# Three chained layers on one core: the last block product of each Strassen run moved into the next run, raw weights in a ring

## Chip, cores and metric

One core of one Trainium2 chip. The metric is the device time in microseconds (us) of one execution, median of the runs; shorter is better.

## What is computed

Sigmoid attention over 24 heads, then a gated MLP with an RMS norm in front, then a second MLP. All inputs and the output are float32 (the weights reach the chip as 8-byte words, two 32-bit halves each):

```
scores = q @ k.T / 8 - log(448);  a = 1 / (1 + exp(-scores));  o = a @ v      # 2 x 12 heads, 448 x 64
x  = o as (896, 768)
xn = x / rms(x) * rms_g
y  = (silu(xn @ w_gate) * (xn @ w_val)) @ w_out        # 768 -> 1536 -> 768
out = (silu(y @ w2_in)) @ w2_out                       # 768 -> 2048 -> 768
```

## The kernel before

Attention runs first (to about 71 us); its matmuls are issued by `scores` (L382) and `attend` (L409). Then come the products, each float32 product made of three fp32r matmuls of 128x128 by 128x448 (high by high, low by high, high by low, `PASSES`). Most products go through Strassen's algorithm in Winograd's form on 2x2 blocks, with seven block products instead of eight. A call of `strassen` (its matmuls are issued by `group`, L798) is one **run**: seven groups of nine matmuls in the order `A11, S1, S2, A12, S3, S4, A22` (names of the weight side). They go to three PSUM banks: `x` takes A11, S2, S3 and A22, `y` takes S1 and S4, `z` takes A12. In between, the partial sums in a bank have to be read before the next group adds to it: ScalarE saves the bank after A11 (`save`, L830, tile `s0`) and S2 waits for that; it saves it after S2 (`s2`) and S3 waits for that; VectorE's add (L836) reads it after S3 and A22 waits for that. Runs: `g1` to `g5` and `v1` to `v5` (gate and value of the first MLP), `i1` to `i7` (second MLP in). At the end of a run without gating, ScalarE applies silu (L865): to block 11, to blocks 00 and 01 together, and to block 10 out of PSUM.

The products with w_out are `o0`, `o1`, `o2` (`mixed`): a plain part (`product`, L747, two double banks `a` and `b`) and a Strassen part on the same banks. `i0` is `mixed` too, `e0` to `e1b` are the second MLP out.

**Weights.** A slab of weights (`raw`, 128x768 words, 768 KB, or 512 KB for a short one) is loaded by SP's queue (L239) into one of two buffers (pool `wraw`). ScalarE rebuilds the exponent into a tile `f` (`exponent`, L257, one of three buffers), ScalarE or VectorE shifts the tail in place (`tail_act`, L265), VectorE merges both (`merge`, L269), and the buffer is free again. Then the Strassen sums are formed (L687 to L709), and each block is split into a high part on ScalarE (L245) and a low part on VectorE (L248), both in a ring of nine tiles `w`. `mac_steps` gives this in seven steps, A22 last.

**What sets the order.** From the norm on, the program is a list of jobs in a `Plan`; when the kernel is built, `Plan.run` plays it with costs per job, takes for each engine the job that is due first among those whose inputs are ready, and writes the instructions in that order. Each engine then executes its list in order. A load counts there as landed `LAG["S"]` = 4.4 us after it is issued, whatever its size; the job behind it is not put on an engine earlier.

```
            e = scalar(1.08 * n, lambda: exponent(s, spare if alt else None), [r], take="alt" if alt else "f")
            end = now + j.cost + LAG[e]
```

Of the kernel before, what the change touches and what calls it, by code (L numbers as in the profile page):

```python
# [39 lines left out]
LAG = {"A": 0.0481, "D": 0.081, "P": 0.165, "S": 4.4, "G": 5.0}  # L40
HOP = {"A": 0.516, "D": 0.3833, "S": 0.4, "G": 0.5}
# [18 lines left out]
class Job:  # L60


    def __init__(self, eng, cost, fn, deps, take, need):
# [3 lines left out]
        self.due, self.ready, self.left = 1e9, 0.0, 0  # L67
        for d in self.deps:
            d.users.append(self)
# [6 lines left out]
class Plan:  # L76
# [37 lines left out]
    def run(self, busy):  # L114
# [8 lines left out]
        for j in reversed(self.jobs):  # L123
            if j.eng != "P":
                j.due = min([u.due for u in j.users + j.users_of_gift], default=1e9) - WAIT[j.eng] * j.cost - LAG[j.eng] - HOP[j.eng]
# [30 lines left out]
        while left:  # L156
# [6 lines left out]
            while again:  # L163
                again = False
                for e in ("P", "D", "A", "S", "G"):
# [17 lines left out]
                    end = now + j.cost + LAG[e]  # L183
# [14 lines left out]
def tile_attention_two_mlps(  # L198
# [12 lines left out]
    wraw = ctx.enter_context(tc.tile_pool(name="wraw", bufs=2))  # L211
# [23 lines left out]

    def load(s):
        raws[s] = wraw.tile([P, 2 * SLAB], U32, tag="raw", name=f"raw{s}")
        n = 2 * wide(s)
        nc.sync.dma_start(raws[s][:, :n], wd[s].bitcast(U32)[:, :n])  # L239

    def load_next():
        load(order.pop(0))
# [7 lines left out]
    def words(s):  # L250
        return raws[s][:, : 2 * wide(s)].rearrange("p (n two) -> p n two", two=2)
# [329 lines left out]
    plan = Plan({"raw": 0, "f": 1, "ring": RING - 8, "alt": 1, "sum": 1, "ps": 0, "one": 0})  # L581
# [57 lines left out]
    wjob = {}  # L639

    def weight_front(s, act_z, tiles, alt=False):
# [3 lines left out]
        r = None if s in LOADED else plan.add("S", 0.4, lambda: load(s), take="raw")  # L645
# [3 lines left out]
        return plan.frees("raw", dve(n, lambda: merge(s), [e, z]))  # L649
# [11 lines left out]
    def weight_mac(macs, act_z, alt=True, early=False):  # L661

        todo = [mac_steps(s, n, act_z, alt, early) for s, n in macs]
        for _ in range(8):
            for t in todo:
                next(t)

    def mac_steps(s, n, act_z, alt, early):
# [24 lines left out]

        s1 = dve(hw, first, m, take=None if inside else "sum")
# [24 lines left out]
        if one:  # L719
            plan.frees("alt" if alt else "f", l1, l2, l4, l5, l6)  # L720
        else:
            if not inside:
                plan.frees("sum", l1, s2)
            plan.frees("f", *[l2, l5] + ([l1] if inside else []))
            plan.frees("alt" if inside else "f", l4, l6)
# [95 lines left out]
    def strassen(name, s, book, fdep, dst, own=None, gate=None):  # L821
# [26 lines left out]
        v1 = save(1, by, g2_)  # L848
        g3 = g(bx, "S2", deps=[v0])
# [4 lines left out]
        g5 = g(bx, "S3", deps=[v2])  # L854
        a11, o11 = output(1, 1, bx, 1, [g5, v1] + ([a00] if dst.fresh else []))
        g6 = g(by, "S4", stop=True, deps=[v1])
        a01, o01 = output(0, 1, by, 2, [g6, v2] + ([a00] if dst.fresh else []))
        by.read_by(v1, a01)
        g7 = g(bx, "A22", stop=True, deps=[a11])
        sdone[:3] = o00, o11, o01  # L860
        if gate:
            e = dve(S, lambda: tt(dst()[:, 1, 0], bx(), dst()[:, 1, 0], ALU.mult), [g7] + gate)
            bx.read_by(e)
            return [o00, o11, o01, e]
        silu = lambda out_, in_: nc.scalar.activation(out_, in_, AF.Silu)  # L865
        d11 = scalar(S, lambda: silu(dst()[:, 1, 1], dst()[:, 1, 1]), [o11])
        d0 = scalar(NT, lambda: silu(dst()[:, 0], dst()[:, 0]), [o00, o01])
        d10 = scalar(S, lambda: silu(dst()[:, 1, 0], bx()), [g7, a00], psum=True)
        bx.read_by(d10)
        return [d11, d0, d10]  # L870

    def mixed(
# [48 lines left out]
        if ahead:  # L921
            a00 = add(0, bz, [g4, v0], 0, 0)
# [655 lines left out]
```

## Time and profile before

| | |
|---|---|
| median of 3 runs | 523.17 us (521.27 to 523.77) |
| the profiled execution | 522.38 us |
| its span, first to last instruction | 520.4 us |
| PE (matmul) busy | 515.3 us, 99%, 2654 matmul records |
| PEld (weight load) busy | 442.7 us, 85% |
| VectorE (DVE) busy | 471.3 us, 91% |
| ScalarE (ACT) busy | 380.5 us, 73% |
| granted TensorE clock | 1.00 |

PE is busy all the time by this page, so a share of busy time tells nothing of a change in the order. What does is the time of one group of nine matmuls in the chain of waits, and whether the weight loader (PEld) had to wait for another engine ahead of a group. The engines' own lists in order of time then tell what that engine did instead.

### The profile page before, as it was taken

The page shows a single profiled execution, that of the slowest core. Times are in us where ns is not written, and L with a number is a line of the kernel's source. Part 1 is how long each engine was busy: PE and PEld are TensorE (multiplying, and loading weights), DVE is VectorE, ACT ScalarE, POOL GpSimd, SP SyncE. Part 2 cuts the span into 40 slices and gives each one's busy share as a digit, 9 for nine tenths or more (in the row PEclk, how much of TensorE's full clock was granted, in tenths as well). Part 3 has the DMA queues.
Part 4 walks back from the last instruction along what each step waited for, and adds up shares of the span by engine and source line. Part 5 has one row for each costly group of instructions (what it writes and reads, how often), then busy time and mean ns, then how long its engine had stood idle before and what let it go on. Part 6 is the DMA issues. An engine that isn't in the chain of part 4 may idle for free.

```text
span 520.4 us, 7479 instructions
## 1 busy us (share of the span) xinstructions
PE 515.3 (99%) x2654; PEld 442.7 (85%) x2654; DVE 471.3 (91%) x883; ACT 380.5 (73%) x677; POOL 13.5 (3%) x28
## 2 busy tenths in 40 slices
PE   9999999999999999999999999999999999999996
PEld 4444469999999999999999999999998999999996
DVE  6799999999999888799989989999988899999992
ACT  6876754787888676876777868998888887778730
POOL 0000000000000000000000000000010101111000
PEclk9999999999999999999999999999999999999999
DMA  8774111033332353411442362333355242555531
GB/s 319 276 248 162 62 62 60 1 122 122 121 123 88 103 209 108 162 42 40 163 161 82 125 217 84 122 121 123 135 186 195 97 134 95 169 199 200 187 123 71
DMA packets 18116, 70.51 MB, mean 136 GB/s; under 512 B 2464, under 2 KB 5024, under 8 KB 18080
## 3 DMA queue, kind: packets, MB, share of 16 engines
q1 hardware_dynamic: 16400, 64.32, 35.8%
q0 software_dynamic: 1536, 5.51, 3.1%
q8 instruction: 20, 0.33, 0.3%
q10 hardware_dynamic: 144, 0.23, 0.1%
q14 instruction: 16, 0.13, 0.1%
HBM read 64.54 MB, written 5.51 MB: 135 GB/s over the span
## 4 chain that ended last, share of the span: by engine, by line
PE 99%; DVE 0%; issue 0%
PE av L409 7%; PE sc L382 6%; PE g L747 3%; PE e2S L798 3%; PE v L747 3%; PE e1x L798 2%; PE o2x L798 2%; PE o1x L798 2%; PE e0bx L798 2%; PE o0x L798 2%; PE e2a L798 2%; PE i6x L798 1%; PE g2x L798 1%; PE i7x L798 1%; PE e0x L798 1%; PE e1bx L798 1%
## 5 line engine op out<-in xcount | busy, mean ns | idle before, releaser
L265 ACT ACTIVATE raw<-raw 128x768 int32<-128x768 uint32 (+1 forms) x70 | 57.4, 825 | 12.9 <-DMA raw<-in_w 9.4
L269 DVE SCALAR_TENSOR_TENSOR f<-f,raw 128x768 uint32<-128x768 uint32 (+1 forms) x65 | 58.4, 900 | 7.5 <-ACT f L257 5.9
L245 ACT ACTIVATE w_S<-f 128x384 fp32r<-128x384 f32 (+1 forms) x90 | 44.7, 497 | 23.0 <-DVE f L698 7.7
L257 ACT ACTIVATE f<-raw 128x768 f32<-128x768 f32 (+1 forms) x65 | 55.7, 859 | 4.4 <-DVE w_S L248 2.6
L248 DVE TENSOR_TENSOR w_S<-f,w_S 128x384 fp32r<-128x384 f32 (+1 forms) x90 | 47.3, 526 | 4.7 <-ACT w_S L245 4.3
L391 ACT ACTIVATE a<-sc,logs 128x896 f32<-128x896 f32 x42 | 39.1, 1008 | 15.3 <-PE sc L382 15.3
L245 ACT ACTIVATE w_A<-f 128x384 fp32r<-128x384 f32 (+1 forms) x84 | 41.2, 500 | 7.2 <-PE o2y L747 1.8
L248 DVE TENSOR_TENSOR w_A<-f,w_A 128x384 fp32r<-128x384 f32 (+1 forms) x84 | 43.8, 533 | 1.8 <-ACT w_A L245 1.8
L409 PE MATMUL av<-a,vr 128*64 128x448 f32 (+1 forms) x192 | 35.4, 552 | 0.0
L409 PEld LDWEIGHTS av<-a,vr 128*64 128x64 f32 (+1 forms) x192 | 10.4, 135 | 21.3 <-issue 20.3
L382 PEld LDWEIGHTS sc<-ks 64*128 64x128 f32 x204 | 18.3, 186 | 10.5 <-issue 5.5
L382 PE MATMUL sc<-ks 64*128 64x448 f32 x204 | 24.7, 380 | 0.0
L1131 DVE TENSOR_TENSOR g<-g 128x448 f32<-128x448 f32 x32 | 19.4, 620 | 0.1
L245 ACT ACTIVATE w_S<-s 128x384 fp32r<-128x384 f32 x24 | 12.5, 520 | 6.0 <-PE g L747 3.1
L709 DVE TENSOR_TENSOR f<-f 128x384 f32<-128x384 f32 (+1 forms) x30 | 15.8, 525 | 0.2
L245 ACT ACTIVATE w_A<-spare 128x128 fp32r<-128x128 f32 (+1 forms) x21 | 7.0, 334 | 12.0 <-DVE spare L269 8.7
L747 PE MATMUL v<-x,w 128*128 128x448 f32 x72 | 15.3, 370 | 0.0
L747 PE MATMUL g<-x,w 128*128 128x448 f32 x72 | 15.3, 368 | 0.0
L747 PEld LDWEIGHTS g<-x,w 128*128 128x128 f32 x72 | 13.4, 188 | 1.7 <-issue 0.7
L747 PEld LDWEIGHTS v<-x,w 128*128 128x128 f32 x72 | 13.5, 188 | 1.4 <-issue 0.4
L248 DVE TENSOR_TENSOR w_S<-s,w_S 128x384 fp32r<-128x384 f32 x24 | 13.3, 552 | 0.9 <-ACT w_S L245 0.9
L687 DVE TENSOR_TENSOR s<-f 128x384 f32<-128x384 f32 x24 | 13.3, 554 | 0.3
(1462 smaller groups left out, 1506.3 us busy)
## 6 DMA issues: line engine op xcount, KB each, us to landing
raw<-in_w SPq DMA_DIRECT2D x52, 768.0 KB, 4.4
raw<-in_w SPq DMA_DIRECT2D x24, 512.0 KB, 3.5
kq<-in_kq SPq DMA_DIRECT2D x11, 448.0 KB, 5.5
out_t<-e SPq DMA_DIRECT2D x8, 224.0 KB, 1.9
vr<-in_v SPq DMA_DIRECT2D x6, 256.0 KB, 4.5
vr<-in_v SPq DMA_DIRECT2D x6, 192.0 KB, 2.5
g_4away<-g POOLq DMA_DIRECT2D x4, 224.0 KB, 2.5
g<-g_4away POOLq DMA_DIRECT2D x4, 224.0 KB, 2.9
```

The source lines that it names most:

```text
L245: nc.scalar.activation(dst, src, AF.Copy)
L248: nc.vector.tensor_tensor(dst, src, hi.bitcast(F32), ALU.subtract)
L257: nc.scalar.activation(floats[s], words(s)[:, :, 1].bitcast(F32), AF.Prelu, scale=2.0**-112, alpha=2.0**32)
L265: nc.scalar.activation(z.bitcast(I32), z, AF.Copy, scale=2.0**-29 * (1 - 2.0**-18), bias=-0.5 + 2.9e-5)
L269: nc.vector.scalar_tensor_tensor(fu, fu, 3, words(s)[:, :, 0], ALU.logical_shift_left, ALU.bitwise_or)
L382: nc.tensor.matmul(ps[to, h, :S], k_[:, keys], q_, start=(step == 0), stop=(step == 2 or plain), skip_group_check=True,)
L391: nc.scalar.activation(a, ps[:, :, :S], AF.Sigmoid, bias=logs, scale=D**-0.5)
L409: nc.tensor.matmul(av[n][h * D : (h + 1) * D, :S], vr[i][rows, c, h, :], a[rows, h, :], start=(begun[n] == 1), stop=(begun[n] == KC + 1), ...
L709: s4 = dve(hw, lambda: tt(block(1), block(1), block(0), ALU.subtract), [s2, l3])
L747: nc.tensor.matmul(banks[b](), t[:, jw], act[key](jx, b), start=(first and i == 0 and n_ == 0), stop=(final and i == n - 1 and n_ == 2), s ...
L798: nc.tensor.matmul(ps(), w[:, jw, j * P : (j + 1) * P], book[t][USES[a]][jx], start=(start and i == 0 and n == 0), stop=(stop and i == len ...
L1131: sub = lambda d, a, b: (lambda: tt(d(), a(), b(), ALU.subtract))
```

## The change

1. `strassen` no longer issues A22 at its end. It leaves it (with what reads the bank behind it) in `late`, and the next run issues it after its own second group: `A11', S1', A22, S2', A12', S3', S4'`. `settle` does this, also after the last run of a layer. In the last run of a layer (`final`) S4 comes ahead of S3.
2. `weight_piped` makes the split blocks in that same order: A22's split is put off until the next run's third step. The `f` tile of the run's second slab is therefore held for longer.
3. The two buffers of raw weights become one ring (`store`) of the same size, in which a short slab takes less room; a load waits for the merges of the slabs that it overwrites. In the plan a load now lands 2.6 + 0.45 per tile of 128 columns after its issue (5.3 us for 768 KB, 4.4 us for 512 KB).
4. `mixed`, plain part first (`o0`, `o1`): the order of the groups is now `A11, A12, S4, S1, S2, A22, S3`, with S4 and A22 added into the double banks; `raw_steps` splits the weights in that order. Bank `b` of `o0` is now read last by the add of block 10.

Every engine has as many instructions as before: 2524 on PE, 883 on VectorE, 676 on ScalarE, 114 loads and stores on SP.

```diff
+LOAD, LOAD_TILE = 2.6, 0.45
...
-                    end = now + j.cost + LAG[e]
+                    end = now + j.cost + j.lag
...
+    store = wraw.tile([P, 4 * SLAB], U32, name="raw")
+    owner, end = [None] * 6, [0]
+
+    def place(s):
+
+        n = 2 * wide(s)
+        at = end[0] if end[0] + n <= 4 * SLAB else 0
+        raws[s], end[0] = store[:, at : at + n], at + n
+        over = {}
+        for k in range(at // (4 * P), (at + n) // (4 * P)):
+            over[owner[k]] = True
+            owner[k] = s
+        return over
...
-        r = None if s in LOADED else plan.add("S", 0.4, lambda: load(s), take="raw")
+        over = [] if s in LOADED else place(s)
+        r = None if s in LOADED else plan.add("S", 0.4, lambda: load(s), [merged[u] for u in over if u is not None])
+        if r:
+            r.lag = LOAD + LOAD_TILE * tiles
...
+    kept = []
+
+    def weight_piped(s, act_z, final=False):
+        steps = piped_steps(s, 3, act_z, True, final)
+        for n in range(7):
+            next(steps)
+            if n == 2:
+                weight_last()
+        kept.append(steps)
+
+    def weight_last():
+        while kept:
+            next(kept.pop())
...
+    def piped_steps(s, n, act_z, alt, early):
...
+        l1 = made("S1", lambda: sums[0], [s1])
+        yield
+        l2 = made("S2", lambda: block(0), [s2])
+        yield
+        l3 = made("A12", lambda: block(1), [m[0]])
+        s4 = dve(hw, lambda: tt(block(1), block(1), block(0), ALU.subtract), [s2, l3])
+        yield
+        for n in range(2):
+            if n == early:
+                l5 = made("S4", lambda: block(1), [s4])
+            else:
+                l4 = made("S3", lambda: block(2), [s3])
+            yield
+        l6 = made("A22", lambda: block(3), [m[1]])
+        frees(l1, l2, l4, l5, l6, s2)
+        yield
...
         v1 = save(1, by, g2_)
+        settle()
         g3 = g(bx, "S2", deps=[v0])
...
-        g7 = g(bx, "A22", stop=True, deps=[a11])
...
+        def last():
+            g7 = g(bx, "A22", stop=True, deps=[a11])
+            if gate:
+                done.append(dve(S, lambda: tt(dst()[:, 1, 0], bx(), dst()[:, 1, 0], ALU.mult), [g7] + gate))
+            else:
+                done.append(scalar(S, lambda: silu(dst()[:, 1, 0], bx()), [g7, a00], psum=True))
+            bx.read_by(done[-1])
+
+        late.append(last)
+        return done
+
+    late = []
+
+    def settle():
+        while late:
+            late.pop()()
...
-            u = save(3, bu, done[-1])
...
+            g6 = g(bv, "S4", stop=True)
...
+            g7 = g(bu, "A22", stop=True)
+            g5 = g(bx, "S3", deps=[v2], stop=True)
+            a11 = add(1, bx, [g5, v1])
+            c11 = add(1, bw, [a11], 1, 1)
+            v3 = save(3, bx, g5)
+            a10 = add(3, bu, [g7, v3], 1, 0)
+            bx.read_by(a11, v3)
+            bb.read_by(c11, a10)
+            return
...
-            weight_mac([(4 * p, 3)], True)
+            weight_piped(4 * p, True)
         silu = strassen(f"g{p}", 4 * p, xbook, xdep, f[p])
...
+    weight_last()
+    settle()
...
-            weight_mac(macs, ZO)
+            weight_mac(macs, ZO, raw_first=True)
```

**The order on PE at the seam of two runs**, `i5` to `i6` (the tile after the comma is the weight side: `w50_S4` is block S4 of slab 50). Before:

```order
L798 MATMUL i5y_3787<-x1h0_1048,w50_S4_3753 128x448 x3
L798 MATMUL i5x_3769<-y0h0_2734,w50_A22_3759 128x448 x3
...
L798 MATMUL i6x_3898<-h3tl1_2457,w52_A11_3762 128x448 x3
...
L798 MATMUL i6y_3916<-y0h0_2734,w52_S1_3824 128x448 x3
...
L798 MATMUL i6x_3898<-y0h1_2656,w52_S2_3839 128x448 x3
```

Now:

```order
L887 MATMUL i6x_3819<-h3tl1_2467,w52_A11_3705 128x448 x3
...
L887 MATMUL i6y_3838<-y2_0_2723,w52_S1_3763 128x448
...
L887 MATMUL i5x_3692<-y2_0_2723,w50_A22_3769 128x448
...
L887 MATMUL i6x_3819<-y0h1_2737,w52_S2_3778 128x448
L887 MATMUL i6x_3819<-h0tl1_1361,w52_S2_3778 128x448
```

Between `i6`'s A11 and its S2 there is now a second group, A22 of `i5`.

**ScalarE at the seam of `v1` and `g2`** (`raw11`, `raw12`: the tail of slabs 11 and 12 in place; `g2s0`: the save after A11 of `g2`; `w8_S4`: high part of a block). Before:

```order
L245 ACTIVATE w8_A12_1337<-f8_1164 128x384
L245 ACTIVATE w8_S3_1340<-f9_1275 128x384
L265 ACTIVATE raw11_1293<-raw11_1293 128x768
L265 ACTIVATE raw12_1313<-raw12_1313 128x768
L245 ACTIVATE w8_S4_1367<-f8_1164 128x384
L830 ACTIVATE g2s0_1369<-g2x_1348 128x448
```

Now (the ring is one tile, `raw_79`):

```order
L281 ACTIVATE raw_79<-raw_79 128x768
L273 ACTIVATE f10_1309<-raw_79 128x768
L261 ACTIVATE w8_S2_1315<-f8_1203 128x384
L261 ACTIVATE w8_A12_1322<-f8_1203 128x384
L281 ACTIVATE raw_79<-raw_79 128x768
L919 ACTIVATE g2s0_1343<-g2x_1317 128x448
L261 ACTIVATE w8_S4_1353<-f8_1203 128x384
```

The tail of slab 12 no longer stands ahead of `g2s0`; two tails in a row have become two with three other instructions between them.

**VectorE at the seam of `o0` and `o1`** (`yr0` is the output of `o0`, `o0b` its bank `b`). Before:

```order
L891 TENSOR_TENSOR o0s1_2471<-o0x_2402,o0s1_2471 128x448
L248 TENSOR_TENSOR h3tl1_2457<-yr0_2515,h3tl1_2457 128x448
L891 TENSOR_TENSOR yr0_2515<-o0b_2343,o0s1_2471 128x448
L248 TENSOR_TENSOR w30_0_2545<-f30_2520,w30_0_2545 128x384
L248 TENSOR_TENSOR w30_1_2551<-f30_2520,w30_1_2551 128x128
L891 TENSOR_TENSOR o0s2_2485<-o0y_2427,o0s2_2485 128x448
L269 SCALAR_TENSOR_TENSOR f31_2553<-f31_2553,raw31_2493 128x768
```

Now:

```order
L996 TENSOR_TENSOR o0s1_2477<-o0x_2374,o0s1_2477 128x448
L996 TENSOR_TENSOR yr0_2506<-o0b_2315,o0s1_2477 128x448
L996 TENSOR_TENSOR yr0_2506<-o0b_2315,o0s3_2555 128x448
L285 SCALAR_TENSOR_TENSOR f31_2565<-f31_2565,raw_79 128x768
L285 SCALAR_TENSOR_TENSOR f32_2581<-f32_2581,raw_79 128x768
```

Bank `b` was read for the last time in the middle of `o0`; now it is by the third add behind `o0`'s last group, and `o1b`, which reuses the bank, comes after that add.

## Rows read from the trace of the kernel before

**Rows 1.** The page: busy time, share of the span and instructions.

```profile
PE 515.3 (99%) x2654; PEld 442.7 (85%) x2654; DVE 471.3 (91%) x883; ACT 380.5 (73%) x677; POOL 13.5 (3%) x28
```

**Rows 2.** Waits of the weight loader from 80 us on: us in total, times, longest.

```profile
PEld g2x L798 <- ACT g2s L830: 0.4, 1, 0.4
PEld v L747 <- issue: 0.4, 2, 0.2
PEld i6x L798 <- ACT i6s L830: 0.3, 1, 0.3
```

**Rows 3.** Chain that ended last, 126 to 136 us: start, us, what.

```profile
127.80 1.82 PE g2x L798 x9
129.62 1.83 PE g2y L798 x9
131.45 0.02 issue
131.47 2.09 PE g2x L798 x9
133.56 1.83 PE g2z L798 x9
```

**Rows 4.** The same chain, 386 to 428 us.

```profile
387.70 1.82 PE i6x L798 x9
389.53 1.82 PE i6y L798 x9
391.35 2.04 PE i6x L798 x9
393.39 1.86 PE i6z L798 x9
...
411.99 1.86 PE i7x L798 x9
413.85 2.48 PE e0x L798 x12
...
421.29 2.48 PE e0x L798 x12
423.77 2.43 PE e0y L798 x12
```

**Rows 5.** ScalarE in order of time, 119 to 133 us: start, us, what [idle before, releaser].

```profile
126.57 0.90 ACT L265 ACTIVATE raw<-raw 128x768 int32<-128x768 uint32 x1
129.67 0.91 ACT L265 ACTIVATE raw<-raw 128x768 int32<-128x768 uint32 x1 [2.20 <-DMA raw<-in_w]
130.47 0.52 ACT L245 ACTIVATE w_S<-f 128x384 fp32r<-128x384 f32 x1
130.88 0.54 ACT L830 ACTIVATE g2s<-g2x 128x448 f32<-128x448 f32 x1
```

**Rows 6.** Loads of raw weights, issue to landing: 121 to 131 us, then 80 to 520 us.

```profile
DMA to landing us min/median/max: 4.5/5.6/6.7
...
DMA to landing us min/median/max: 3.3/4.3/6.7
```

**Rows 7.** ScalarE in order of time, 384 to 392 us.

```profile
386.16 0.90 ACT L265 ACTIVATE raw<-raw 128x768 int32<-128x768 uint32 x1 [1.15 <-DMA raw<-in_w]
...
388.96 0.52 ACT L865 ACTIVATE g<-i5x 128x448 f32<-128x448 f32 x1
389.38 1.40 ACT L865 ACTIVATE g<-g 128x896 f32<-128x896 f32 x2
390.69 0.52 ACT L830 ACTIVATE i6s<-i6x 128x448 f32<-128x448 f32 x1
```

**Rows 8.** Busy time of a stretch: PE (count), PEld, DVE, ACT, POOL, clock, DMA.

```profile
200.00:220.00 20.00, 20.00 (x101) 18.53 (x100) 17.12 (x30) 14.50 (x27) 0.00 (x0) 1.00 0.44 142
```

**Rows 9.** All engines in order of time, 256 to 262 us, seam of `o0` and `o1`.

```profile
256.62 0.36 PE L798 MATMUL o0x<-h3th,w_A 128*128 128x448 f32 x1
257.13 0.62 DVE L891 TENSOR_TENSOR yr<-o0x,o0s 128x448 f32<-128x448 f32 x1
258.40 0.96 DVE L269 SCALAR_TENSOR_TENSOR f<-f,raw 128x768 uint32<-128x768 uint32 x1 [0.18 <-ACT raw L265]
259.25 1.78 PE L747 MATMUL o1b<-x,w 128*128 128x448 f32 x8
260.28 0.62 DVE L1131 TENSOR_TENSOR yr<-yr 128x448 f32<-128x448 f32 x1
260.81 0.55 DVE L695 TENSOR_TENSOR f<-f,f 128x384 f32<-128x384 f32 x1
```

**Rows 10.** Waits of ScalarE, whole kernel: us in total, times, longest.

```profile
ACT raw L265 <- DMA raw<-in_w: 9.4, 7, 2.4
```

**Rows 11.** Groups of instructions from 80 to 516 us: count | busy us, mean ns | idle before.

```profile
L257 ACT ACTIVATE f<-raw 128x768 f32<-128x768 f32 x45 | 40.5, 903 | 2.6 <-DVE w_S L248 1.9 <-DMA raw<-in_w 0.5
L248 DVE TENSOR_TENSOR w_A<-f,w_A 128x384 fp32r<-128x384 f32 x71 | 38.4, 552 | 0.3 <-ACT w_A L245 0.3
```

**Rows 12.** The chain that ended last: two pieces of the whole, early and last.

```profile
80.37 7.30 PE v L747 x36
...
514.36 1.84 PE e1bx L798 x9
```

More of the change, by code (lines that the diff above doesn't have):

```diff
@@ L124, in run @@
             if j.eng != "P":
-                j.due = min([u.due for u in j.users + j.users_of_gift], default=1e9) - WAIT[j.eng] * j.cost - LAG[j.eng] - HOP[j.eng]
+                j.due = min([u.due for u in j.users + j.users_of_gift], default=1e9) - WAIT[j.eng] * j.cost - j.lag - HOP[j.eng]
         free = dict(busy)
@@ L579, in tile_attention_two_mlps @@
     pools = {"T": tp, "F": fp, "x": xp, "r": rp, "e": ep}
-    plan = Plan({"raw": 0, "f": 1, "ring": RING - 8, "alt": 1, "sum": 1, "ps": 0, "one": 0})
+    plan = Plan({"f": 1, "ring": RING - 8, "alt": 1, "sum": 1, "ps": 0, "one": 0})
     tt = nc.vector.tensor_tensor
@@ L692, in made, with frees, mac_steps @@
             return wjob[s, a]
+        def frees(l1, l2, l4, l5, l6, s2):
+            if one:
+                plan.frees("alt" if alt else "f", l1, l2, l4, l5, l6)
+            else:
+                if not inside:
+                    plan.frees("sum", l1, s2)
+                plan.frees("f", *[l2, l5] + ([l1] if inside else []))
+                plan.frees("alt" if inside else "f", l4, l6)
+        return hw, one, inside, m, sums, block, first, made, frees
+    def mac_steps(s, n, act_z, alt, early):
+        hw, one, inside, m, sums, block, first, made, frees = mac_blocks(s, n, act_z, alt, early)
         s1 = dve(hw, first, m, take=None if inside else "sum")
@@ new lines, in raw_steps @@
+    def raw_steps(s, n, act_z, alt, early):
+        hw, one, inside, m, sums, block, first, made, frees = mac_blocks(s, n, act_z, alt, early)
+        s1 = dve(hw, first, m, take=None if inside else "sum")
+        s3 = dve(hw, lambda: tt(block(2), block(0), block(2), ALU.subtract), [s1, m[0]])
+        yield
+        l0 = made("A11", lambda: block(0), [m[0]])
+        s2 = dve(hw, lambda: tt(block(0), sums[0], block(0), ALU.subtract), [s3, l0])
+        yield
+        l3 = made("A12", lambda: block(1), [m[0]])
+        s4 = dve(hw, lambda: tt(block(1), block(1), block(0), ALU.subtract), [s2, l3])
+        yield
+        l5 = made("S4", lambda: block(1), [s4])
+        yield
+        l1 = made("S1", lambda: sums[0], [s1])
+        yield
+        l2 = made("S2", lambda: block(0), [s2])
+        yield
+        l6 = made("A22", lambda: block(3), [m[1]])
+        yield
+        l4 = made("S3", lambda: block(2), [s3])
+        frees(l1, l2, l4, l5, l6, s2)
@@ L910, in mixed @@
                     )
-            u = save(3, bu, done[-1])
-        else:
-            bx, by, bz, bw = (Banks(f"{name}{c}") for c in "xyzw")
+            v0 = save(0, bx, g(bx, "A11", start=True, stop=True, first=bx))
+            a00 = add(0, bz, [g(bz, "A12", stop=True), v0], 0, 0)
+            g6 = g(bv, "S4", stop=True)
+            g2_ = g(by, "S1", start=True, stop=True, first=by)
+            v1 = save(1, by, g2_)
+            g3 = g(bx, "S2", deps=[v0])
+            v2 = save(2, bx, g3)
+            a01 = add(2, by, [g2_, v2])
+            by.read_by(v1, a01)
+            c01 = add(2, bv, [a01, g6], 0, 1)
+            ba.read_by(a00, c01)
+            g7 = g(bu, "A22", stop=True)
[7 more added lines that the diff above has]
+            return
+        bx, by, bz, bw = (Banks(f"{name}{c}") for c in "xyzw")
         g1 = g(bx, "A11", start=True, first=bx)
@@ L1391, in tile_attention_two_mlps @@
         if t < 2:
-            weight_mac(macs, ZO)
-        macs = [(macs[0][0], range(3)), (macs[1][0], (3,))]
+            weight_mac(macs, ZO, raw_first=True)
+        macs = [(w, range(3) if n == 3 else (3,)) for w, n in sorted(macs)]
         mixed(
```

121 lines of the change are left out of this document (58 added, 63 removed).

## Prediction

> **What bounds the kernel now.** I read the page first: PE is busy 99% of the span, PEld 85% [rows 1]. Then the chain of waits, which is PE from end to end after 80 us, and in it the time of one group of nine matmuls: 1.82 or 1.83 us, alternating, so 1.825 us, or 0.203 us a matmul [rows 3]. The same 0.203 holds in the opening products (36 in 7.30 us) and in the last group [rows 12]. PE is therefore bound by its own stream of matmuls, and since the changed program has the same 2524 of them, only what departs from that pace can be won. The waits of the weight loader show how little that is: from 80 us on it waited for another engine twice, 0.4 and 0.3 us [rows 2].
>
> Both are the same wait: S2 of a run adds to the bank that ScalarE must have saved after A11, in `g2` and in `i6`. ScalarE's list tells why it was late. In `g2` it stood 2.20 us at the tail of a slab whose load had not landed, with a split and the save `g2s` queued behind [rows 5]; the two loads took 4.5 and 6.7 us to land, the second behind the first [rows 6], where the plan had counted 4.4. In `i6` it stood 1.15 us for a load, and then three silus of `i5` (0.52 and 1.40 us) were ahead of the save, which began at 390.69 us, 1.16 us after the A11 group had given way to S1 [rows 4, 7]. Over the kernel ScalarE waited 9.4 us for loads in seven waits [rows 10]; five of them cost PE nothing.
>
> **The change, part by part.** The sum is made against the profiled execution, 522.38 us (span 520.4 and 2.0 around it). The median of the runs shown is 0.8 us above it.
>
> *The seam of two runs.* Before, one group (S1, 1.825 us) lay between A11 and S2, and in it the save had to start, last 0.52 to 0.54 us [rows 5, 7] and be seen. Now S1 and the old run's A22 lie between: 3.65 us. ScalarE may come 1.8 us later than before without PE noticing. The two stalls were 0.29 us (131.45 to 133.56 is 2.11 us for a group of 1.825 [rows 3]) and 0.22 us (2.04 less 1.825 [rows 4]), so both fit in the new room six times over. Gain **0.51 us**. The same move gives VectorE's add ahead of A22 two more groups as well; nobody waited there, so it is worth nothing.
>
> *The pace after the second stall.* Behind it the groups take 1.86 us instead of 1.825 (eleven of them, 393.39 to 413.85), then 2.48 instead of 2.43 (four of twelve matmuls), and at 423.77 the old pace is back [rows 4], all at a granted clock of 1.00. That is 11 x 0.035 + 4 x 0.05 = **0.59 us**. It began with the stall, and I take it to go with it. From the other side: after the first stall the pace stayed at 1.825 to 1.83 [rows 3], so a slow stretch is no certain companion of a stall and might come without one. Ends: 0 and 0.59 gained; I take 0.59, since the only slow stretch after 80 us starts exactly at a stall.
>
> *Loads.* The plan now counts 5.3 us for a 768 KB load, where the median landing of all is 4.3 us and the worst 6.7 us [rows 6]. Its work on ScalarE is put 0.9 us later; a lone load is then there in time, one behind another can still be 1.4 us late. That is under the 1.8 us of new room at the seam, so I cost it at 0. If the cover is gone (the save after S2 still has only A12's 1.825 us in front of S3): less the save (0.54) and the hand-over from PE (0.15, from 256.98, the end of a matmul, to 257.13 [rows 9]) there are 1.1 us, and a tail that is 1.4 us late ahead of such a save stalls PE by 0.3 us each time. On SP's queue a load now waits for the merges of the slabs that it overwrites, as it did by buffers; SP itself has nothing else to do in this stretch.
>
> *The f tile held for longer.* The `f` tile of a run's second slab comes free with A22's split, now needed two groups later. The next slab that takes it is two runs on; from A22 in the third place of a run to the next run's A11 there are five groups, 9.1 us, and exponent, merge, high and low of A11 take 0.90 + 0.96 + 0.52 + 0.55 = 2.9 us [rows 5, 9, 11]. Cost 0.
>
> *The seam of `o0` and `o1`.* S3 is now the last group of `o0`, and behind it come three adds before bank `b` is free. With T the start of S3's last matmul: the first add starts at T + 0.51 (256.62 to 257.13), the adds follow at 0.53 us (260.28 to 260.81), and the third ends at T + 0.51 + 1.06 + 0.62 = T + 2.19 [rows 9]. `o1b` is due at T + 2.63 (256.62 to 259.25 [rows 9]). Room 0.44 us, nothing of VectorE's stands between the adds in the new order; cost 0, or 0.5 us if VectorE is one merge (0.96 us) late.
>
> *The end* has the same last instructions on PE and VectorE: 0.
>
> Sum: 522.38 - 0.51 - 0.59 = **521.3 us**. The fastest run shown, 521.27, is what an execution without those stalls would give, which fits; it also says that I expect no run much below it.
>
> *Is there more in PE?* The loader is busy 18.53 of 20 us where PE ran 101 matmuls and nobody waited [rows 8]: the missing 7% is no wait, it is how 0.185 us loads stand in a stream of one per 0.2 us. The Trainium skill, Perfetto Trace Analysis, "Identifying the Most-Contended Engine", says that matmul busy time is no good measure of the distance to the roofline and that the busy share of weight loads is. By that, 520.4 - 442.7 = 77.7 us would be headroom and an order with fewer gaps could win many microseconds; by the rows 1.1 us. The trace does not agree that the missing share can be won by order.
>
> **The rivals.**
>
> *The loads still decide (about 522.4).* The waits do not go, they move: a tail that waits for its load ends up ahead of a save after S2, or the seam of `o0` and `o1` stalls. For it: ScalarE had five more waits for loads [rows 10], and landings reach 6.7 us. Against: 0.9 us more margin per load. Three stalls of 0.3 to 0.5 us give back what is won: 522.0 to 523.0.
>
> *PE falls into its slow pace for long (slower).* The stream has two paces, 1.825 and 1.86 us a group [rows 4]. With fewer stalls there are fewer points at which it changes; if it starts slow at the opening products and nothing disturbs it, it stays slow. From 80.37 to 516.2 us that is 435.8 x 0.035 / 1.825 = 8.4 us: 529.7 us. It decides from about 240 us of slow stretch on. Against: in the trace 30 us of 436 were slow, and only behind a stall.
>
> *Weights come late (slower).* The `f` tile is the place: if ScalarE and VectorE have more than 6.2 us of other work between A22's split and the next A11, PE waits at the start of a run. At 0.5 us for each of 17 runs: 529.8 us. Against: ScalarE is idle 27% of the span [rows 1], and 2.9 us of work has 9.1.
>
> *More is won than the profiled execution shows.* The runs shown reach up to 523.77, so other executions lose more to late loads than the profiled one; a median may move by 1.9 us (to 521.3) though the profile shows 1.1. Below 520.5 needs a gain that no row shows.
>
> *PE has headroom that order can fill.* A tenth of the loader's idle 77.7 us would be 7.8 us: 514.6. The page named above stands behind it; the stretch without waits [rows 8] speaks against it.
>
> **How the numbers follow.** Both stalls gone and none new, 520.5 to 522.0: 0.70. Loads still decide, 522.0 to 523.4: 0.14. Slow pace 0.04, late weights 0.03. More won, under 520.5: 0.08, headroom 0.01. The predicted time is the first case's, 521.3. The range 520.4 to 523.3 takes in the first two cases, with the bounds of the pace (0.59) and of the new stalls; it leaves out some 0.18. About 0.5% (2.6 us) is what a measurement of this kernel can tell from no change; against 523.17 that is 520.6 to 525.8. So faster 0.10 (the last two cases and the lower edge of the first), slower 0.07, within it 0.83.
>
> **What the new profile would show.** Right: no wait of the loader for ScalarE after 80 us; groups of 1.825 us throughout, no stretch at 1.86; `g2s` and `i6s` saved well ahead of S2; fewer or shorter waits of ScalarE for loads than 9.4 us; a span near 519.3 us. Wrong: a new wait of PE at S3 for the save after S2, or at `o1b` for VectorE; a stretch at 1.86 us without a stall ahead of it; a fall of the time by more than 2 us with PE's group time unchanged.

## The result, and the profile after

The changed kernel takes 525.07 us (median of 12 runs, 523.73 to 527.95), the kernel before on the same chip 522.47 us (12 runs): a ratio of 1.0058, 95% interval 1.0038 to 1.0079. It is slower by 2.6 us, where 521.3 was predicted. The profiled execution is 524.96 us, its span 523.1. All medians here take in every execution; a ratio leaves out an execution that took over 1.5% longer than the fastest of its kernel.

The page of the changed kernel, busy time of each engine:

```profile
PE 515.9 (99%) x2654; PEld 443.9 (85%) x2654; DVE 470.3 (90%) x883; ACT 381.1 (73%) x677; POOL 13.5 (3%) x28
```

Beside [rows 1] nothing stands out. The waits of the weight loader from 80 us on (us in total, times, longest) tell more:

```profile
PEld e0x L887 <- ACT e0s L1079: 2.4, 1, 2.4
```

The two waits of [rows 2] are gone, and one of 2.4 us has come. The chain that ended last, at the two old stalls and at the new one (start, us, what):

```profile
131.31 1.83 PE g2x L887 x9
...
390.92 1.82 PE i6x L887 x9
...
418.61 2.52 issue
421.13 3.76 DMA g<-g_4away
...
424.91 0.58 ACT g4B L261
425.49 0.56 ACT f L273
426.04 0.46 ACT g4B L261
426.50 0.44 ACT e0s L1079
...
426.99 3.79 PE e0x L887 x12
430.78 2.90 PE e0w L887 x12
```

`g2x` and `i6x` run at 1.82 to 1.83 us, where [rows 3, 4] had 2.09 and 2.04, and the 1.86 us groups behind `i6x` [rows 4] are gone too. Ahead of e0's S3 PE waits for the save `e0s` behind S2; ScalarE comes to it late, because a split `g4B` ahead of it waited for a quarter of `g4` that POOL was fetching back from DRAM. (`g4` is an output tile of the layer ahead; the program moves it out to DRAM, `g_4away`, and POOL's queue brings it back in four quarters of 224 KB ahead of `e0`.) ScalarE in order of time (start, us, what [idle before, releaser]), first of the kernel before, then of the changed one:

```profile
421.93 1.05 ACT L245 ACTIVATE g4B<-g 128x448 fp32r<-128x448 f32 x2 [1.03 <-DMA g<-g_4away]
```

```profile
424.91 0.58 ACT L261 ACTIVATE g4B<-g 128x448 fp32r<-128x448 f32 x1 [3.24 <-DMA g<-g_4away]
...
426.41 0.53 ACT L1079 ACTIVATE e0s<-e0x 128x448 f32<-128x448 f32 x1
```

POOL's own list shows why the quarter came so late, first of the kernel before, then of the changed one:

```profile
409.29 0.55 POOL L1237 DMA_DIRECT2D g<-g_4away  x1 [21.80 <-PE i7x L798]
412.75 0.56 POOL L1237 DMA_DIRECT2D g<-g_4away  x1 [2.91 <-issue]
...
419.08 0.56 POOL L1237 DMA_DIRECT2D g<-g_4away  x1 [2.61 <-issue]
```

```profile
409.37 0.55 POOL L1345 DMA_DIRECT2D g<-g_4away  x1 [23.69 <-PE i7x L887]
414.97 0.56 POOL L1345 DMA_DIRECT2D g<-g_4away  x1 [5.05 <-issue]
...
421.13 0.56 POOL L1345 DMA_DIRECT2D g<-g_4away  x1 [2.52 <-issue]
```

The four quarters go one after the other, the next issued when the one before has landed, though the profile shows no wait of POOL for another engine or a transfer between them (`issue`). The first took 5.3 us in the changed kernel, where it had taken 3.2, and pushed the others back by 2.1 us. The issues between 409.0 and 409.8 us show its company, those between 420.6 and 421.8 us that of the fourth (KB each, us to landing):

```profile
raw<-in_w SPq DMA_DIRECT2D x1, 768.0 KB, 4.3
raw<-in_w SPq DMA_DIRECT2D x1, 512.0 KB, 6.0
g<-g_4away POOLq DMA_DIRECT2D x1, 224.0 KB, 5.3
...
raw<-in_w SPq DMA_DIRECT2D x1, 512.0 KB, 3.5
g<-g_4away POOLq DMA_DIRECT2D x1, 224.0 KB, 3.8
```

The fourth took 3.8 us where it had taken 2.8. The last quarter therefore landed 3.0 us later than before (424.89 and 421.91 us): 2.1 us come from the first fetch and 0.9 from the fourth.

Behind the stall PE is slow for a while. PE by stretches (length, busy and count, granted clock, DMA share, GB/s):

```profile
425.00:427.00 2.00, 0.01 (x1) 1.00 0.31 115
428.00:431.00 3.00, 3.00 (x11) 0.55 0.88 326
432.00:436.00 4.00, 4.00 (x22) 1.00 0.53 176
```

The granted clock fell from 2.4 to 1.2 GHz for most of 428 to 431 us (and for part of the next microsecond, 0.66 there). The account: PE's chain from its first gate matmul to its end is 448.03 us (70.78 to 518.81), before 445.22 (70.98 to 516.20), that is 2.8 more. By the starts of matmuls, S3 was due at 424.81 us (S4 began at 422.37 and has 12 x 0.2027 us) and began at 426.99: 2.18 us of stall. The 24 matmuls from there on took 6.53 us, to 433.52, instead of 24 x 0.2027 = 4.86: 1.66 us behind it. Up to S4 the changed kernel had won 1.0 us, of the 1.1 that were foreseen.

What the clock takes seems to differ between executions of this one kernel. By the mean granted clock of each, three executions at 0.999 took 523.7 to 524.3 us, four at 0.997 took 524.6 to 525.2, and three at 0.995 took 526.4 to 526.5; the two slowest, 527.72 at 1.000 and 527.95 at 0.997, do not fit this row. This is a hint and no measure: a mean can also fall at the end of the span, where PE has finished, and only one of the twelve was profiled.

### The profile page after: what moved, and what is told of

Its sections match the earlier page's. It is cut to its first block, busy times and chain, and to the rows that moved or that the text cites. A ratio compares the mean times of both kernels' runs of the same rounds, so it can differ in the third digit from the quotient of the medians.

```text
span 523.1 us, 7442 instructions
## 1 busy us (share of the span) xinstructions
PE 515.9 (99%) x2654; PEld 443.9 (85%) x2654; DVE 470.3 (90%) x883; ACT 381.1 (73%) x677; POOL 13.5 (3%) x28
## 4 chain that ended last, share of the span: by engine, by line
PE 96%; issue 2%; DMA 1%; ACT 0%; POOL 0%; DVE 0%
PE av L425 7%; PE sc L398 6%; PE g L836 3%; PE v L836 3%; PE e2S L887 3%; PE e1x L887 2%; PE e0bx L887 2%; PE e2a L887 2%; PE o2x L887 2%; PE e1bx L887 1%; PE i3x L887 1%; PE v4x L887 1%; PE g2x L887 1%; PE i5x L887 1%; PE i4x L887 1%
## 5 line engine op out<-in xcount | busy, mean ns | idle before, releaser
L261 ACT ACTIVATE w_S<-f 128x384 fp32r<-128x384 f32 (+1 forms) x90 | 43.3, 496 | 25.2 <-DVE f L756 6.4
L264 DVE TENSOR_TENSOR ks<-kq,ks 128x896 fp32r<-128x896 f32 (+2 forms) x14 | 13.1, 949 | 0.4
L261 ACT ACTIVATE w<-f 128x384 fp32r<-128x384 f32 (+1 forms) x22 | 9.4, 460 | 5.5 <-PE o2x L836 1.9
```

The source lines that it names most:

```text
L261: nc.scalar.activation(dst, src, AF.Copy)
L264: nc.vector.tensor_tensor(dst, src, hi.bitcast(F32), ALU.subtract)
```

## The experiments

**The theory.** POOL's quarters of `g4` come one after the other; the loads that the new order and ring put beside the first make all of them late; ScalarE stands at `g4B` with the save behind it; PE waits, and the clock falls. Rivals: ScalarE's new order is late by itself, or the interleaving is.

**Quarters of g4 on SP's queue.** Nothing else is moved.

```diff
-                    nc.gpsimd.dma_start(self.got[1][:, m, b], home[:, m, b])
+                    queue = nc.sync if self.name == "g2_4" else nc.gpsimd
+                    queue.dma_start(self.got[1][:, m, b], home[:, m, b])
```

> The changed kernel, but g4's four quarters come back from DRAM on SP's queue instead of POOL's; the orders on PE, ScalarE and VectorE stay as they are. Theory (POOL brings the quarters one after the other, and the loads that the new order puts beside them make each later): the last quarter lands well before 421 us, ScalarE no longer stands 3.24 us ahead of g4B, the wait of PE at e0x (2.4 us) and the 3.4 us at a granted clock of 0.5 are gone: 525.07 - 2.2 - 1.7 = 521.2, between 520.9 and 521.8 us. Rival 1 (ScalarE's place in the new order is late by itself, not the fetches): the wait at e0x stays at 2 us or more, 524 to 526 us. Rival 2 (the quarters fall behind the 768 KB loads on SP's queue and make those late): waits of ScalarE for raw loads grow past 4.2 us in sum, a new stall of 0.5 to 2 us, 522 to 524 us.

Measured: 520.17 us, 0.9966 of the kernel before (0.9937 to 0.9995); profiled 519.97. No wait of the loader is left from 80 us on. The fetches of this line, and their issues (KB each, median us to landing):

```profile
L1346 SPq DMA_DIRECT2D g<-g_4away x4: 331/431/645, 408.6 to 411.1; - x4
...
g<-g_4away SPq DMA_DIRECT2D x4, 224.0 KB, 5.7
```

Each takes 5.7 us (median), longer than most on POOL's queue, but four are on their way at once: all are there by about 411.1 + 5.7 = 416.8 us instead of 424.9. Both rivals fall, since the orders on ScalarE and PE are those of the changed kernel and the stall is gone. The time is under the 520.9 to 521.8 us that were expected. PE's chain is 70.42 to 514.57 us here, 444.15, that is 1.07 less than before: the 1.10 that the prediction worked out, once the stall does not eat it. The rest of the 2.4 us to the profiled execution of before lies outside this chain: 0.6 us ahead of it, 0.55 at the end (the span ends 2.98 us after VectorE's last add, before 3.53) and 0.2 outside the span.

**PE kept busy in the gap.** Ten matmuls between e0's S4 and S3.

```diff
+            def fill():
+                t = ps_tile("fill")
+                for j in range(10):
+                    nc.tensor.matmul(t[:, j % 2, :S], square, row, start=True, stop=True)
+
+            plan.add("P", 0.0, fill)
```

> The changed kernel, with ten matmuls of 128 x 448 added between S4 and S3 of e0, into a bank that nobody reads; they only fill the time in which PE stands there. Theory (the stall is 2.2 us of waiting, and 1.7 us more because the clock is granted at 0.5 for 3.4 us behind the gap): the wait for ScalarE's save stays, the granted clock stays at 1.00, 525.07 - 1.7 = 523.4, between 523.0 and 523.8 us. Rival (the slower matmuls behind the stall do not come from the gap): 3.4 us at a granted clock of 0.5 stay although PE was busy, 525 us or more.

Measured: 523.54 us, 1.0029 (1.0011 to 1.0047); profiled 523.31, 1.65 below the changed kernel. The save is as late as before, and the clock stays (the chain, then the stretch behind the gap; `fill` itself runs from 424.18 us):

```profile
426.40 0.44 ACT e0s L1079
...
426.89 2.70 PE e0x L887 x12
429.59 2.43 PE e0w L887 x12
```

```profile
427.00:432.00 5.00, 5.00 (x25) 1.00 0.63 232
```

The 24 matmuls behind the gap take 4.97 us (426.89 to 431.86) instead of 6.53. So 1.6 us of the loss was the clock behind the gap, and matmuls that compute nothing win it back. That the whole execution is shorter by nearly the same 1.65 us is in part a coincidence: its wait is 0.5 us longer (S3 was due at 424.18), and its first gate matmul comes 0.55 us earlier.

**One fetch more in the kernel before.**

```diff
-                    nc.gpsimd.dma_start(self.got[1][:, m, b], home[:, m, b])
+                    for _ in range(2 if (self.name, m, b) == ("g2_4", 0, 0) else 1):
+                        nc.gpsimd.dma_start(self.got[1][:, m, b], home[:, m, b])
```

> The kernel before, with the first quarter of g4 brought from DRAM twice, so that POOL has five fetches of 224 KB in a row there instead of four. Theory (the fetches go one after the other at 2.8 to 3.2 us, and the order before had only 0.2 us of room at e0): the last quarter lands some 2.9 us later, near 424.8 us, ScalarE stands some 3.9 us ahead of g4B, PE waits 2.4 to 3 us ahead of e0's S3 with half clock behind it: 522.5 + 4 = 526.5, between 525 and 527.5 us. Rival (the fetches run beside each other, and a fifth costs nothing): within 0.3 us of 522.5.

Measured: 527.13 us, 1.0082 (1.0046 to 1.0118); profiled 524.90. The chain through POOL, and behind the two old stalls:

```profile
391.02 1.98 PE i6x L798 x9
393.00 1.83 PE i6z L798 x9
...
418.20 0.55 POOL g L1238
418.75 2.58 issue
421.33 2.85 DMA g<-g_4away
...
424.20 1.04 ACT g4B L245 x2
425.25 0.44 ACT e0s L971
...
425.73 2.30 PE e0y L798 x10
```

One more fetch in the row is a stall at e0 in the old order too: the kernel before had no room there. In its trace the load for `e0y` behind the save comes 0.26 us after the load ahead of it, where 0.20 is usual:

```profile
423.20 0.19 PEld L798 LDWEIGHTS e0x<-lone,w_S 128*128 128x128 f32 x1
423.46 0.54 PEld L798 LDWEIGHTS e0y<-g0B,w_S 128*128 128x128 f32 x3
```

The second fetch of the same quarter waits for the first by a semaphore (2.8 us on POOL), which the edit brings with it; the three behind it wait for nothing that the profile shows, and still go one at a time. Three things differ from the theory. The stall is ahead of e0's S4, behind the save after S1. In this execution the loader stood for 3.3 us and the clock stayed at 1.00 behind it; the mean granted clock is 1.000 in four of the eight executions (524.3 to 526.6 us) and 0.995 to 0.997 in the other four (527.7 to 532.3), so the profile may show only one of two outcomes. And the groups behind `i6x` stay at 1.82 to 1.83 us, though `i6x` stalls as it did in [rows 4].

**All returning tiles on SP's queue,** and counted there as loads by the plan.

```diff
-                    nc.gpsimd.dma_start(self.got[1][:, m, b], home[:, m, b])
+                    nc.sync.dma_start(self.got[1][:, m, b], home[:, m, b])
...
-                    jobs.append(plan.add("G", 1.2, back(m, b), gone, need=ready))
+                    jobs.append(plan.add("S", 0.4, back(m, b), gone, need=ready))
```

> The changed kernel with all tiles that come back from DRAM (g4 and those of e0 and e1) on SP's queue, and counted there as loads when the order is made (0.4 us of the queue, landed 4.4 us after the issue). Theory (the serial fetches are the only new loss): no wait of PE over 0.5 us after 80 us, 520.9 to 521.8 us. Rival (a new order moves the loads of weights, and some land late): a new stall of 0.5 us or more, 522 to 524 us.

Measured: 520.41 us, 0.9962 (0.9948 to 0.9975), again under the range expected, and no wait of the loader from 80 us on.

**The plan told when the quarters land.** They stay on POOL.

```diff
                     jobs.append(plan.add("G", 1.2, back(m, b), gone, need=ready))
+                    if self.name == "g2_4":
+                        jobs[-1].lag = (4.1, 5.8, 7.5, 10.3)[n]
```

> The changed kernel, with one thing told to the plan: that the four quarters of g4 land 5.3, 8.2, 11.1 and 15.1 us after the first is issued, as they did in the changed kernel, in place of 6.2 to 9.8. They stay on POOL's queue. PE's order is the same; on ScalarE the save e0s after S2 now stands ahead of the two splits g4B that wait for the quarters. Theory (the loss is the save's place behind that wait): the fetches stay as late as 424 to 425 us and ScalarE may wait for them, but no wait of PE over 0.5 us: 520.2, between 519.8 and 521.2 us. Rival (the late quarters themselves hold PE up, the save only stood in the same place): PE waits 1 us or more for g4B inside S3, 521.5 to 525 us.

Measured: median 521.22 us, 0.9966 (0.9937 to 0.9996). ScalarE in the profiled execution:

```profile
426.11 0.55 ACT L1079 ACTIVATE e0s<-e0x 128x448 f32<-128x448 f32 x1
426.55 0.58 ACT L261 ACTIVATE g4B<-g 128x448 fp32r<-128x448 f32 x1
429.49 0.58 ACT L261 ACTIVATE g4B<-g 128x448 fp32r<-128x448 f32 x1 [2.37 <-DMA g<-g_4away]
```

The save now stands ahead, ScalarE still waits 2.37 us for a quarter, and the loader has no wait for another engine: the loss was the save's place behind the wait. But this execution took 526.36 us. Its whole excess is pace: from `o1b` on, at 259 us, a matmul takes 0.2067 us instead of 0.2027. Another one took 526.82, the other ten 520.6 to 522.2.

**The two loads beside the first quarter made thin.**

```diff
-        nc.sync.dma_start(raws[s], wd[s].bitcast(U32)[:, : 2 * wide(s)])
+        n = 2 * wide(s) // (8 if s in (60, 61) else 1)
+        nc.sync.dma_start(raws[s][:, :n], wd[s].bitcast(U32)[:, :n])
```

> The changed kernel, in which the two loads of raw weights that go out beside g4's first quarter bring an eighth of their bytes (96 KB and 64 KB; the rest of these two slabs is old data, so seven eighths of two slabs of weights are left out). Theory (the pair of loads made the first quarter take 5.3 us where 2.9 is usual, and three quarters stand behind it): the first quarter takes 2.8 to 3.2 us, the last lands near 422.5 us, ScalarE's wait for it falls from 3.2 to about 1 us, PE waits under 0.3 us at e0: 520.2 to 521.2 us. Rival (the quarters are slow for another reason): the first takes 4 us or more, the stall stays above 1.5 us, 523 us or more.

Measured: 520.66 us, 0.9955 (0.9931 to 0.9980). The fetches on POOL run from 408.7 to 418.2 us by issue, and who waited for them:

```profile
L1346 POOL DMA_DIRECT2D g<-g_4away x4: 548/556/560, 408.7 to 418.2; - x4
...
ACT g4B L262: 0.2, 1
```

The last quarter is issued 9.5 us after the first, not 11.8, and PE does not wait. (One thin load, overwriting less, also went out 6 us ahead of the quarter.) So it is the loads beside the fetches that turned a row of them that had just been fast enough into one that was not. The fourth fetch, too, takes 2.9 us here; how much of the 3.0 us each of the two meetings alone would cost PE, this run does not tell.

**The ring undone,** the new order kept.

```diff
-        at = end[0] if end[0] + n <= 4 * SLAB else 0
-        raws[s], end[0] = store[:, at : at + n], at + n
+        at = end[0]
+        raws[s], end[0] = store[:, at : at + n], 2 * SLAB - at
```

> The changed kernel without the ring: raw weights in two fixed halves again, each load waiting for the merges of its half; order of the groups as changed. Theory (the ring lets two loads go out together just where g4's first quarter is fetched): no two loads are issued within 1 us of each other beside that fetch, it takes about 3 us, and PE's wait for the save after S2 of e0 is under 1 us; some loads are later in turn, so another stall of up to 1.5 us may come at e0's first groups: 520.5 to 522.5 us. Rival (the interleaved order alone brings the stall): a wait of 2 us or more for a save of e0 stays, 524 us or more.

Measured: 525.22 us, 1.0038 (1.0013 to 1.0062); expected were 520.5 to 522.5. The first quarter takes 2.9 us as foreseen, but the second meets another load, ScalarE waits 1.8 us at `g4B`, and PE 1.1 us for a save of e0; weights that now come later stall it elsewhere (1.6 us at `e2S`, 1.7 at `e0x`). The time is the one that the rival named, the wait at e0 is not. This run does not tell ring and order apart: without the ring the order loses more than it wins.

**The kernel before with g4's quarters on SP's queue.** The edit is the first one's.

> The kernel before with g4's four quarters on SP's queue; the orders on the other engines stay. Both stalls that the change removes are left in (g2 and i6). Theory (the interleaved order by itself is worth some 0.5 to 1.1 us, and what made runs of the kernel before so different is the same chain of quarters, with 0.2 us of room): no wait of PE at e0, waits of the loader of 0.2 to 0.4 us at g2x and i6x, runs within 1.5 us of each other, median 520.8 to 521.6 us, that is 0.5 to 1.1 above the changed order with the same queue. Rival (all of the gain of that version comes from the queue and the order is worth nothing): within 0.2 us of 520.3.

Measured: 521.49 us, 0.9968 (0.9942 to 0.9995), and on another chip 520.84 us, 0.9966 (0.9943 to 0.9990). The chain at the old stall:

```profile
390.67 2.09 PE i6x L798 x9
392.76 1.82 PE i6z L798 x9
```

Here too the groups behind the stall run at 1.82 us. That its executions would lie within 1.5 us of each other did not hold (3.2 us and 1.7, but for one each over 525). The second time it ran beside the interleaved version with all returning tiles on SP:

> The kernel before with g4's quarters on SP's queue once more, on the same chip as the run ahead. Theory (the interleaved order is worth the stalls that are left here, 0.3 to 0.5 us in the profiled execution, and more in executions with late loads): 0.4 to 1.2 us above the run ahead. Rival (the order is worth nothing once the quarters come early): within 0.2 us of it.

> The version with all returning tiles on SP's queue once more, on one chip with the next. Theory (no wait of PE after 80 us, and the order keeps it so in every execution): median 520.2 to 520.8 us, runs within 1.5 us of each other, save one in ten that runs at the slower pace of matmuls.

That version gave 520.75 us, 1.0001 (0.9970 to 1.0031), where one slow execution in ten was expected: seven lie from 519.8 to 520.8 us and five from 525.3 to 526.0, all at a granted clock of 1.00. As the runs stand, it is 0.1 us under the 520.84 of the old order, and the rival (the order is worth nothing once the quarters come early) is not refuted. The seven alone have a median of 520.36, 0.5 us under it, as the profiles have it (519.97 with the new order and 520.49 with the old, quarters on SP's queue in both). So 0.5 us is what the interleaving seems worth where the five do not come; the five ask for a cause of their own.

**The slow pace.** Of this version's 60 executions (five sets of twelve, the other three below) 9 are over 525 us: 0, 5, 0, 1 and 3 by set. One of the nine was profiled (525.78 us), the others are taken to be like it by their time; its chain at the seam of `o0` and `o1`:

```profile
256.44 2.44 PE o1a L836 x12
258.87 2.47 PE o1b L836 x12
261.35 2.48 PE o1a L836 x12
```

The pace turns at the first group of `o1b` and stays: 1.86 us a group of nine at 400 us. It turns in the same place in the execution of 526.36 us above. VectorE's last adds on `o0`, and the loader's rows there:

```profile
256.67 0.62 DVE L996 TENSOR_TENSOR o0s<-o0x,o0s 128x448 f32<-128x448 f32 x1
257.32 1.20 DVE L996 TENSOR_TENSOR yr<-o0b,o0s 128x448 f32<-128x448 f32 x2
```

```profile
256.07 2.42 PEld L836 LDWEIGHTS o1a<-x,w 128*128 128x128 f32 x12
258.58 1.35 PEld L836 LDWEIGHTS o1b<-x,w 128*128 128x128 f32 x7
```

Twelve loads from 256.07 us end at 256.07 + 12 x 0.203 = 258.50, where the first of `o1b` is due; it starts at 258.58, when the adds are through (258.52). It is 0.08 us late, which the loader's slack all but hides: PE loses 6 ns. This lateness is in all ten profiles of the new order with the ring, at either pace (without the ring the load is on time); it is the seam that the change made. The last edit takes it away, by putting two groups of `o1` on bank `a` ahead of the first on bank `b`:

```diff
-            for k in range(0, n, 2):
-                for m, t in enumerate((ba, bb)):
-                    i = 2 * k + 2 * m
-                    done += product(
+            pairs = [(k, m) for k in range(0, n, 2) for m in range(2)]
+            if name == "o1":
+                pairs[1:3] = pairs[2:0:-1]
+            for k, m in pairs:
+                t, i = (ba, bb)[m], 2 * k + 2 * m
+                done += product(
```

> The version with all returning tiles on SP's queue, and the first two groups of o1's plain part in bank a ahead of the first in bank b, so that bank b of o0, which now is read until 2.45 us after S3's last matmul began, is needed 2.4 us later. Theory (in the changed order the first weight load of o1b comes 75 to 80 ns late in every profile, which costs PE 6 ns, but in some executions tips it to 0.2067 us a matmul for the rest, 256 us, that is 5 us): no late load at o1b, no execution over 521.5 us, median 520.3 us (519.8 to 520.8). Rival 1 (the slow pace comes by itself): some executions at 525 to 526.5 us as without the swap. Rival 2 (it comes from another place, with any short wait): the same, with the switch elsewhere in the trace.

> The version with all returning tiles on SP's queue a third time, beside the run ahead. Theory: executions of two kinds, some at 519.8 to 521 us and some (0 and 5 of 12 in the two runs so far) at 525.3 to 526 us; a profile of the second kind shows 0.2067 us a matmul from 258 us on.

Measured: 520.07 us, 0.9928 (0.9898 to 0.9959), all twelve from 519.7 to 520.9; without the swap 520.25 us, 0.9945 (0.9920 to 0.9970), and none over 525 us on this chip either, so this did not yet tell the two apart. The pair was run twice more:

> The version with the swap in o1 once more. Theory (the slow pace is tipped by the load of o1b that comes 75 to 80 ns late, which the swap removes): all executions under 521.5 us. Rival (it comes by itself): about one in nine at 525 to 526.5 us, as in the versions of the new order without the wait at e0 (8 of 70 executions so far).

> As the second run of the version with the swap in o1. Theory: all executions under 521.5 us. Rival (the slow pace comes by itself): about one in nine at 525 to 526.5 us.

With the swap 520.33 us, 0.9953 (0.9936 to 0.9970), and 520.27 us, 0.9944 (0.9918 to 0.9971), nothing over 521.13; without it 520.40 us, 0.9969 (0.9949 to 0.9989), with one execution over 525, and 520.54 us, 0.9964 (0.9928 to 0.9999), with three. In sum 0 of 36 against 9 of 60. If the swap did nothing, 36 executions in a row would all miss a chance of 0.15 each 0.3 times in 100; but that counts executions of one set as independent, and they come in clusters. Of the three pairs run side by side alone, 0 of 36 against 4 of 36, a split like this would come by luck some 6 times in 100. Together with the place at which the pace turns in both profiles, this points to the late load; it does not prove it. Nor is that load the only way to such times: the old order with the quarters on SP's queue, where it is not late, has one execution over 525 us in each of its two runs (528.40 and 526.28, at a granted clock of 1.00), neither of them profiled. With the swap no load of `o1b` is late any more, and the loader waits for no other engine from 80 us on. This version beats both kernels: 520.1 to 520.3 us, against 522.6 to 522.9 of the kernel before beside it.

## Why the prediction was wrong

*The seam of two runs* (gain 0.51): right. Both waits are gone. In the four profiles of the old order the one at `i6x` is always there, 0.3 to 0.6 us on the loader, whatever queue the quarters take; the one at `g2x` is in two of them.

*The pace after the second stall* (gain 0.59): the slow stretch was not there in the new profile, but the reason was wrong. The same stall at `i6x` left the pace alone in three other profiles of the old order, and in two of the new order the slow pace came where the loader's list shows no wait for another engine, only a load 0.08 us late. That it goes with the stall was taken from one instance; the working's own lower end (0, "might come without one") was the right one for the change, and that the profiled execution of before was slow there was luck.

*Loads* (cost 0): **the step that failed.** It said that SP has nothing else to do in this stretch. So it is, but POOL has: four fetches of 224 KB, which took 2.8 to 3.2 us each in the kernel before and up to 5.3 us beside the loads of the new order. The step left out these fetches and ScalarE's wait for them altogether. The step did price a late transfer ahead of a save after S2, but only tails of weights, at 0.3 us each. In the trace of before ScalarE already waited 1.0 us at `g4B` ahead of a save of e0, and no room was left behind that wait. The wait stands in the list of ScalarE's waits, but the working follows only those for raw weights there. It cost 3.8 us now: 2.18 us of stall and 1.66 at half the clock, for which the sum had no term.

*The f tile held for longer* (cost 0): right; no start of a run waits for weights.

*The seam of o0 and o1* (room 0.44 us, cost 0): wrong, and not for its size alone. The working took the time at which `o1b`'s first matmul is due; its weight load, which waits for the bank, is due 0.2 us earlier. The first add begins 0.60 us behind the start of S3's last matmul (256.07 us in the profile of 525.78 us), not 0.51. The three adds take 1.85 us, from 256.67 to 258.52, not 1.68. And the load begins 0.06 us behind their end. So the room was -0.08 us, not 0.44. In the profiled execution that cost 6 ns; in some others of this order PE turns to its slow pace at this very place, for the 256 us that are left, 5 us.

*The end* (cost 0): right; the last pieces on PE and VectorE are the same. The 0.6 us that the span is shorter behind them goes with the fetches on SP (2.9 to 3.0 us behind the last add with g4's quarters on SP's queue, 3.5 to 3.7 with them on POOL's, in old and new order), not with this change; why is open.

*The rivals.* "The loads still decide" was the mechanism, ScalarE held by a transfer ahead of a save after S2, with the wrong transfer and too low a price, since it foresaw three waits of 0.3 to 0.5 us. "PE falls into its slow pace for long" is real: it had a chance of 0.04, and by their times one execution in seven of a version without the stall has it, at 5 us instead of 8.4, because it starts at 258 us and not at 80. "Weights come late" did not come. "More is won than the profiled execution shows" is not what the 520.2 to 520.4 us with the quarters on SP's queue stand for: the same queue gives the old order 520.8 to 521.5. "PE has headroom that order can fill" is now answered on the chip: with the swap in `o1` the loader waits for no other engine from 80 us on, and it is still busy only 443.0 of 518.8 us, 85% as in [rows 1]. Of the 75.8 us in which it is idle 39.9 lie ahead of 80 us, in the attention, with matmuls of other shapes; from 100 to 500 us it is busy 370.8 of 400 us, 93%. The Trainium skill, Perfetto Trace Analysis, "Identifying the Most-Contended Engine", judges headroom on this engine by MFU (the share of the peak rate of arithmetic) and by the busy share of the weight loads. Here the 7% that are left in that stretch stand where nothing is waited for, so this run shows no room in them that another order could win.

**What stays open.** Why the fetches on POOL's queue go one at a time (the program is built with `dynamic_dma_scratch_size=256`, which no run varied); why a gap of 2.4 us cost the clock in the profile of the changed kernel and one of 3.3 us did not in the kernel with a fetch more, and whether executions of one kernel differ in this, as their mean clocks suggest; whether it is the late load that tips the pace, and why in some executions only; whether the changed kernel's two executions at 527.7 and 528.0 us have the slow pace as well, since neither was profiled.

## What to carry to other kernels

List every transfer that an engine's queue waits for, on every DMA queue, and how much room each wait has in the trace, ahead of moving loads: a wait that costs nothing may have no room left behind it, as here, where it came to cost 3.8 us. Transfers of one queue may run one at a time; several small ones that are due together belong where they can be on their way at once. On a stream of matmuls without gaps, work out when the weight load is due, not the matmul, and read the pace ahead of and behind each late load.

## What the runs showed of the hardware

- Fetches of 224 KB on POOL's queue went one at a time, 2.8 to 3.2 us each in the kernel before and 0.3 us from a landing to the next issue; beside two loads of 768 and 512 KB one took 5.3 us. Four on SP's queue were on their way together and took 5.7 us each (median), 8.2 us in all where POOL took 12.6 in the kernel before.
- Behind the gap of 2.4 us the granted clock was at its lower level for most of 3 us; in the profile with ten matmuls in the gap it stayed at 1.00, and so it did behind a gap of 3.3 us in another version. What made the difference is open.
- The stream of fp32r matmuls of 128x128 by 128x448 has two lasting paces at a granted clock of 1.00: 0.2027 and 0.2067 us. In two profiles it turned from the first to the second at a weight load 0.08 us late and nothing later turned it back; in eight others with the same late load it did not turn. In the kernel before it ended at e0 [rows 4], at the load that is 0.06 us late there.
